# Attention into MoE: the sums of squares move from VectorE and GpSimd to ScalarE and GpSimd

## The chip, the cores and the metric

The kernel runs on one core of a Trainium2 chip. The metric is device time in microseconds (us), lower is better. A core has five engines that run their own instruction queues in order: TensorE (PE, with its weight loads shown as PEld), VectorE (DVE), ScalarE (ACT), GpSimd (POOL) and SyncE (SP), which here issues every DMA.

## The reference

Random-feature attention feeds a mixture of experts. What matters here is the feature map `phi`, made for every row of q and k.

```python
def phi(x):                                   # x: batch 4, heads 8, rows 576, head_dim 64
    proj = np.einsum('bhsd,md->bhsm', x, omega)          # m = 128 features
    sq = np.sum(x * x, axis=-1, keepdims=True) / 2.0
    h = proj - sq
    h = h - np.max(h, axis=-1, keepdims=True)
    return np.exp(h) / np.sqrt(m)
q_p, k_p = (phi(q_s), phi(k_s))               # q_s, k_s = q * scale, k * scale, scale = 64 ** -0.25
kv = np.einsum('bhsm,bhsd->bhmd', k_p, v)
z = np.sum(k_p, axis=2)
num = np.einsum('bhsm,bhmd->bhsd', q_p, kv)
den = np.einsum('bhsm,bhm->bhs', q_p, z)[..., None] + 1e-06
x = num / den                                 # 2304 tokens of 512
# MoE: 8 experts of 512 -> 1024 -> 512, gates normalised by 8 Sinkhorn rounds
for e in range(8):
    out += P[:, e:e + 1] * (np.maximum(x @ w1[e], 0.0) @ w2[e])
```

## The kernel before

**Two parts.** The attention part makes the 2304 tokens and ends at about 175 us. The MoE part, from about 192 us to the end, is a long stream of matmuls of split-precision operands, on 16 units (expert, half of its hidden width).

**Jobs.** Attention is cut into 36 jobs, 0 to 35, written out in `jobs`: 18 k jobs and 18 q jobs. A job takes one half of the heads of one loaded tile (`k`, `q`, or the remainders `kr`, `qr`); a tile of 128x1024 serves two jobs. Jobs 0 to 4 are k jobs, 5 to 30 alternate k and q, 31 to 35 are q jobs. Each runs as a generator whose stages are advanced by `tick`, so several jobs overlap.

**A job on the engines.** PE transposes the tile (`tp`, L327); ACT or DVE copies the result to SBUF (`th`, L330 or L332); PE multiplies by omega (`pp`, L339, 16 matmuls, one such group in each job); DVE takes the negated maxima into one column of `sqs` (L342) and adds the three columns of `sqs` to the shift `cn` (L344); half of the exponentials are made by ACT with that shift as bias (L352), the other half by DVE's addition (L354) and ACT's exponential (L355). A k job then multiplies with v (`kv`, L364); a q job transposes, multiplies with `kvs` and divides.

**The sums of squares.** `squares` writes, for one tile, two columns of `sqs`: the sum of squares times c and times -c (they cancel in the sum of three columns when the maximum, which stands between them, is taken over the projection alone). Tile 0 is squared by ACT (L300). All others are squared by GpSimd (L302) and folded in halves by GpSimd down to 8 columns (L305); DVE ends the sum (L306) and makes the two scaled columns (L307, L308). `ensure_loads` calls `load` and `squares` ahead of the job that needs them.

**What sets the order.** A scheduler that simulates a timeline sets each engine's order from the order of the code and the dependencies; work with no dependency that holds it can be drawn forward. `last_cn` is used for ties: a GpSimd copy of 8 columns of the newest `cn` into a tile makes what fills that tile wait for that job.

**Weights.** `stage` loads weights of a unit, `split` makes their high and low parts (ACT copies `wh`, GpSimd or DVE subtracts to `wl`, L223); unit 0's first weights are handled inside the attention part. The tokens of a chunk (three chunks of 6 tiles) are split by ACT (L125), DVE (L126) and GpSimd (L110) and stored to DRAM as `xd`.

Of the kernel before, what the change touches and what calls it, by code (L numbers as in the profile page):

```python
# [9 lines left out]
F32 = mybir.dt.float32  # L10
F32R = mybir.dt.float32r
AF = mybir.ActivationFunctionType
ALU = mybir.AluOpType
AX = mybir.AxisListType
# [8 lines left out]
def moe_attention_kernel(  # L23
# [23 lines left out]
    nc = tc.nc  # L47
    B, H, S, D = q.shape
    M = omega.shape[0]
    N, DM = out.shape  # L50
    E = w_gate.shape[1]
    FF = w1.shape[2]
    P = 128
    KD = DM // P
# [25 lines left out]
    def bank(name):  # L80
        return ps[0].tile([P, 512], F32, tag="b", name=name)
# [9 lines left out]
    ORDER = [1, 5, 6, 3, 7, 2, 4]  # L91
# [77 lines left out]
    last_cn = []  # L169
# [58 lines left out]
    sc = sc_cm.__enter__()  # L228
    rw_cm = tc.tile_pool(name="rw", bufs=1, side="right", reuse_waits="tile")
    rw = rw_cm.__enter__()  # L230
# [12 lines left out]
    wgs = sc.tile([P, KD, GC], F32, name="wgs")  # L243

    def prepare_gate():

        nc.gpsimd.memset(wgs, 0.0)
        wg = sc.tile([P, KD, E], F32, name="wg")
        nc.sync.dma_start(out=wg, in_=w_gate.rearrange("(k p) e -> p k e", p=P))
        nc.vector.tensor_copy(wgs[:, :, :E], wg)  # L250

    rawt = {}
    vts = [rw.tile([P, H, 2 * D + 2], F32, name=f"v{i}") for i in range(4)]
    for t in vts:
        nc.gpsimd.memset(t[:, :, 0 :: 2 * D + 1], 1.0)
    nv = [0]

    def load(which, key):

        src = {"q": q, "k": k, "v": v}[which]  # L260
        is_v = which == "v"
        if key[0] == "r":
            pr = key[1]
            rows = [(slice(i * SR, (i + 1) * SR), 2 * pr + i) for i in range(2)]
            if is_v:
                t = rw.tile([P, H, D + 1], F32, tag="vr", bufs=1, name="vr")
                nc.gpsimd.memset(t[:, :, :1], 1.0)
                o = t[:, :, 1:]
            else:
                t = rw.tile([P, H, 1, D], F32, tag=f"{which}r", bufs=1, name=f"{which}r")  # L270
                o = t[:, :, 0, :]
            for r, b in rows:
                nc.sync.dma_start(out=o[r], in_=src[b, :, SM:S, :].rearrange("h p d -> p h d"))
            rawt[which, key] = t
            return
        b, half = key
        view = src[b, :, :SM, :].rearrange("h (p j) d -> p h j d", j=JM)[:, :, 2 * half : 2 * half + 2, :]
        if is_v:
            t = vts[nv[0] % 4]
            nv[0] += 1  # L280
            nc.sync.dma_start(out=t[:, :, 1 : 2 * D + 1].rearrange("p h (j d) -> p h j d", j=2), in_=view)
        else:
            t = rw.tile([P, H, 2, D], F32, tag=which, bufs=4, name=which)
            nc.sync.dma_start(out=t, in_=view)
        rawt[which, key] = t

    sqt = {}
# [3 lines left out]
    def squares(which, key):  # L291

        t = rawt[which, key]
        n = 1 if key[0] == "r" else 2
        s = sc.tile([P, H, n, D], F32, tag="sq", bufs=2, name="sq")
        o = sc.tile([P, H, n, 3], F32, tag="sqs", bufs=8, name="sqs")
        c = 1.0 / (2.0 * math.sqrt(D))
        w = D
        if not sqt:
            nc.scalar.activation(s, t[:, :H], AF.Square)  # L300
        else:
            nc.gpsimd.tensor_tensor(s, t[:, :H], t[:, :H], op=ALU.mult)  # L302
            while w > 8:
                w //= 2
                nc.gpsimd.tensor_tensor(s[..., :w], s[..., :w], s[..., w : 2 * w], op=ALU.add)  # L305
        nc.vector.tensor_reduce(o[..., 1], s[..., :w], axis=AX.X, op=ALU.add)  # L306
        nc.vector.tensor_scalar_mul(o[..., 0], o[..., 1], c)  # L307
        nc.vector.tensor_scalar_mul(o[..., 2], o[..., 1], -c)  # L308
        sqt[which, key] = o

    kvs = {}
# [8 lines left out]
    def feature_stages(which, key, hh, on_act):  # L320


        tin = rawt[which, key].rearrange("p h j d -> p (h j d)")
        tp = bank("tp")
        for i in range(4):
            o = (4 * hh + i) * P
            nc.tensor.transpose(tp[:, i * P : (i + 1) * P], tin[:, o : o + P], ident)  # L327
        th = sc.tile([P, 4, P], F32, tag="th", bufs=2, name="th")
        if which == "k" and len(sqt) > 4:
            nc.scalar.copy(th.rearrange("p a s -> p (a s)"), tp)  # L330
        else:
            nc.vector.tensor_copy(th.rearrange("p a s -> p (a s)"), tp)  # L332
        yield
        hs = sqt[which, key].rearrange("p h j t -> p (h j) t")[:, 8 * hh : 8 * hh + 8]
        pp = [bank("pp") for _ in range(2)]
        for i in range(4):
            for g in range(2):
                r = slice(g * D, (g + 1) * D)
                nc.tensor.matmul(pp[g][:, i * M : (i + 1) * M], lhsT=th[r, i], rhs=omt[r], start=True, stop=True)  # L339
        p3 = [p.rearrange("p (h m) -> p h m", h=4) for p in pp]  # L340
        for g in range(2):
            nc.vector.tensor_reduce(hs[:, g::2, 1], p3[g], axis=AX.X, op=ALU.max, negate=True)  # L342
        cn = sc.tile([P, 8], F32, tag="cn", bufs=4, name="cn")
        nc.vector.tensor_reduce(cn, hs, axis=AX.X, op=ALU.add)  # L344
        last_cn.append(cn)
        res = []
        for g in range(2):
            ex = sc.tile([P, 4, M], F32, tag="ex", bufs=8, name="ex")
            c4 = cn[:, g::2]
            if on_act and g == 1:  # L350
                for i in range(4):
                    nc.scalar.activation(ex[:, i, :], p3[g][:, i, :], AF.Exp, bias=c4[:, i : i + 1])  # L352
            else:
                nc.vector.tensor_tensor(ex, p3[g], c4.unsqueeze(2).to_broadcast([P, 4, M]), op=ALU.add)  # L354
                nc.scalar.activation(ex, ex, AF.Exp)  # L355
            res.append(ex)
        yield
        yield
        return res
# [370 lines left out]

    def ensure_loads(i):
        for it in list(need):
            if it[0] <= (i + 1 if it[1] == "v" else i + 3):
                need.remove(it)
                load(it[1], it[2])
                if it[1] != "v":
                    sq_todo.append(it)
        while sq_todo and sq_todo[0][0] <= i + 2:
            _, w, key = sq_todo.pop(0)
            squares(w, key)  # L740

    sq_todo = []
# [9 lines left out]

    ensure_loads(0)
    for i, jb in enumerate(jobs):
        if i == 4:
            prepare_gate()
        if i == 8:
            stage(0, 1)
        if i >= 14 and i % 2 == 0 and (i - 14) // 2 < 7:
            split(0, 1, ORDER[(i - 14) // 2])  # L760
        if i == 24:
            stage(0, 2)
        gen = k_job(jb[1], jb[2]) if jb[0] == "k" else q_job(*jb[1:])
        active.append((jb, gen))
        tick()
        ensure_loads(i + 1)
# [25 lines left out]
    for s, (u, n) in enumerate(steps):  # L792
        c = n // (CT // 2)
# [11 lines left out]
        for k, i in enumerate(ORDER):  # L805
# [3 lines left out]
            if k < ((5, 5, 4) if s > 2 else (3, 4, 3))[n % 3] and todo:  # L809
                pc = todo.pop(0)  # L810
                first(*pc)
                j = ORDER.index(pc[2])
# [44 lines left out]
```

## Time and profile before

| what | value |
| --- | --- |
| time, three runs | 1652.38, 1653.94, 1654.0 us; median 1653.94 us |
| the profiled execution | 1653.92 us, with a span of 1652.1 us from its first to its last instruction |
| PE busy | 96% of the span |
| DVE busy | 85% |
| ACT busy | 46% |
| POOL busy | 19% |

The shares are means over both parts. The MoE part is nearly all of the span, so they say little of the attention part, in which each engine's share is a different one.

### The profile page before, as it was taken

How to read it: one execution, taken by the hardware profiler on the slowest of the kernel's cores; microseconds unless marked ns; L12 is line 12 of the kernel's file. 1: busy time of each engine (PE TensorE's matmuls, PEld its weight loads, DVE VectorE, ACT ScalarE, POOL GpSimd, SP SyncE). 2: the span in 40 equal slices, each digit the busy share in tenths (PEclk: the TensorE clock that was granted, in tenths of full speed). 3: DMA queues.
4: the chain of work that ended last, by engine and by line, in shares of the span. 5: the costliest groups of instructions: out<-in, count | busy, mean ns of one | idle time of the engine just before them, and what ended most of it. 6: DMA issues, size and time to landing. Idle time of an engine off the chain costs nothing.

```text
span 1652.1 us, 31432 instructions
## 1 busy us (share of the span) xinstructions
PE 1591.1 (96%) x12318; PEld 1556.0 (94%) x12318; DVE 1412.3 (85%) x2779; ACT 759.9 (46%) x1373; POOL 316.9 (19%) x259
## 2 busy tenths in 40 slices
PE   5799889999999999999999999999999999999998
PEld 4678679999999999999999999999999999999997
DVE  6988779898979898889888888989898888889877
ACT  2577655444434344443544443444444444444333
POOL 7871141111102011111111120102111111101003
PEclk8899999999999999999999999999999999999999
DMA  9423576665665655566657565665665565655562
GB/s 231 110 83 137 207 282 238 201 221 172 239 208 198 210 204 206 209 217 215 218 175 256 169 219 200 218 210 206 209 218 206 203 229 184 214 189 192 176 226 77
DMA packets 105314, 329.79 MB, mean 200 GB/s; under 512 B 14800, under 2 KB 43984, under 8 KB 105168
## 3 DMA queue, kind: packets, MB, share of 16 engines
q1 hardware_dynamic: 105168, 327.79, 58.5%
q8 instruction: 98, 1.61, 0.4%
q14 instruction: 48, 0.39, 0.1%
HBM read 306.53 MB, written 21.23 MB: 198 GB/s over the span
## 4 chain that ended last, share of the span: by engine, by line
PE 82%; DVE 12%; POOL 2%; DMA 1%; issue 1%; ACT 1%; SPq 0%; DVEq 0%; ACTq 0%; POOLq 0%
PE hx L553 23%; PE x L654 22%; PE hz L553 17%; PE z L654 11%; PE w L654 5%; PE pp L339 2%; DVE out L680 2%; DVE sm L590 2%; DVE sqs L342 1%; DVE bl L590 1%; DVE wl L223 1%; POOL sq L305 1%; DVE sl L629 1%; POOL sq L302 1%; PE np L439 1%
## 5 line engine op out<-in xcount | busy, mean ns | idle before, releaser
L553 PE MATMUL hx<-xs,wh 128*128 128x384 f32 x1536 | 373.2, 337 | 2.0 <-ACT xs L125 1.4
L680 DVE SCALAR_TENSOR_TENSOR out<-x,prob,out 128x256 f32<-128x256 f32 x497 | 233.3, 476 | 66.2 <-PE x L654 64.7
L553 PE MATMUL hz<-xs,wh 128*128 128x384 f32 x1152 | 281.0, 336 | 3.5 <-ACT hr L572 1.4
L553 PEld LDWEIGHTS hx<-xs,wh 128*128 128x128 f32 x1536 | 270.1, 189 | 4.3 <-issue 3.7
L190 POOL TENSOR_TENSOR st<-st 128x512 f32<-128x512 f32 x80 | 131.9, 1649 | 702.3 <-DVE wl L223 699.7
L553 PEld LDWEIGHTS hz<-xs,wh 128*128 128x128 f32 x1152 | 202.2, 188 | 4.9 <-ACT hr L572 1.6
L553 PE MATMUL hx<-xs,wl 128*128 128x384 f32 x768 | 199.7, 336 | 0.0
L632 ACT ACTIVATE bh<-hr 128x512 fp32r<-128x512 f32 x144 | 91.2, 634 | 223.2 <-PE x L654 218.2
L680 DVE SCALAR_TENSOR_TENSOR out<-z,prob,out 128x256 f32<-128x256 f32 x252 | 120.0, 476 | 58.0 <-PE z L654 57.2
L222 ACT CAST wh<-st 128x512 fp32r<-128x512 f32 x176 | 105.0, 621 | 112.7 <-PE hx L553 45.0
L628 ACT CAST sh<-sm 128x512 fp32r<-128x512 f32 x144 | 89.6, 622 | 139.0 <-PE z L654 99.3
L553 PE MATMUL hz<-xs,wl 128*128 128x384 f32 x576 | 150.4, 335 | 0.0
L553 PEld LDWEIGHTS hx<-xs,wl 128*128 128x128 f32 x768 | 139.0, 189 | 0.0
L590 DVE SCALAR_TENSOR_TENSOR sm<-hr,sm 128x256 f32<-128x256 f32 x288 | 135.0, 469 | 2.7
L223 DVE TENSOR_TENSOR wl<-st,wh 128x512 fp32r<-128x512 f32 x169 | 120.6, 724 | 15.1 <-ACT wh L222 14.7
L590 DVE SCALAR_TENSOR_TENSOR bl<-hr,bh 128x512 fp32r<-128x512 f32 x144 | 119.1, 827 | 3.5 <-ACT bh L632 3.3
L654 PE MATMUL z<-wh,sh 128*128 128x256 f32 x576 | 117.7, 281 | 2.8 <-ACT sh L611 2.7
L654 PE MATMUL x<-wl,sh 128*128 128x256 f32 x576 | 118.3, 281 | 0.0
L654 PE MATMUL x<-wh,sh 128*128 128x256 f32 x576 | 117.5, 285 | 0.7 <-DVE out L680 0.6
L654 PE MATMUL z<-wh,sl 128*128 128x256 f32 x576 | 115.5, 282 | 1.6 <-DVE sl L612 1.6
L602 ACT ACTIVATE ah<-hr 128x256 fp32r<-128x256 f32 x144 | 60.3, 419 | 123.3 <-PE x L654 98.0
L654 PE MATMUL z<-wl,sh 128*128 128x256 f32 x576 | 117.0, 281 | 0.0
(155 smaller groups left out, 3507.8 us busy)
## 6 DMA issues: line engine op xcount, KB each, us to landing
xs<-xd SPq DMA_DIRECT2D x329, 768.0 KB, 4.4
st<-in_moe_w_dram SPq DMA_DIRECT2D x64, 512.0 KB, 4.8
xd<-xs SPq DMA_DIRECT2D x21, 768.0 KB, 4.3
k<-in_k_dram SPq DMA_DIRECT2D x8, 512.0 KB, 6.3
v<-in_v_dram SPq DMA_DIRECT2D x8, 512.0 KB, 6.2
q<-in_q_dram SPq DMA_DIRECT2D x8, 512.0 KB, 6.3
out_dram<-out SPq DMA_DIRECT2D x32, 128.0 KB, 1.9
kr<-in_k_dram SPq DMA_DIRECT2D x4, 128.0 KB, 5.8
```

What stands on the lines that cost most here:

```text
L190: nc.gpsimd.tensor_tensor(o, a, b, op=op)
L222: nc.scalar.copy(hi, o)
L223: (nc.vector if u > 0 or (w == 2 and i in (1, 6, 7, 4)) else nc.gpsimd).tensor_tensor(lo, o, raw(hi), op=ALU.subtract)
L302: nc.gpsimd.tensor_tensor(s, t[:, :H], t[:, :H], op=ALU.mult)
L339: nc.tensor.matmul(pp[g][:, i * M : (i + 1) * M], lhsT=th[r, i], rhs=omt[r], start=True, stop=True)
L553: nc.tensor.matmul(pb, lhsT=a[:, k, g * P : (g + 1) * P], rhs=x[:, b, k, :], start=i in (1, 5, 2) and j == 0, stop=j == len(prods) - 1, sk ...
L590: nc.vector.scalar_tensor_tensor(o, in0=a, scalar=0.0, in1=b, op0=ALU.max, op1=op)
L602: nc.scalar.activation(ah, a11, AF.Relu)
L628: nc.scalar.copy(sh, sm)
L632: nc.scalar.activation(bh, a[:, 1:], AF.Relu)
L654: nc.tensor.matmul(pb, lhsT=ops[s][i][a][:, f], rhs=wt[u, 2, i][b][:, f], start=bool(start) and j == 0, stop=j == len(prods) - 1, skip_gro ...
L680: nc.vector.scalar_tensor_tensor(o, in0=pb, scalar=p, in1=o, op0=ALU.mult, op1=ALU.add)
```

## The change

- `squares`: every tile is squared by ACT (L298 in the new file), with a scale that puts the factor c into the square. GpSimd folds from 64 columns down to 2 (L302), adds the last two straight into `sqs` (L303) and writes the negated column (L304). DVE has no part in it. From the first `cn` on, a GpSimd copy (L297) from the newest `cn` into the tile `sq` stands ahead of ACT's square: the tie.
- `feature_stages`: all copies `th` of k jobs are ACT's; the first four were DVE's.
- `ensure_loads`: loads are called for 2 jobs ahead (v) and 5 (q, k) in place of 1 and 3; squares 2 ahead up to job 7, then 4.
- The weights of unit 0: `stage(0, 1)` moves from job 8 to 16, the seven `split` calls from jobs 14 to 26 to jobs 22 to 34, `stage(0, 2)` from job 24 to 30.
- The gate weights are loaded straight into `wgs`, at job 12; the tile `vr` is made and its ones set once.

```diff
@@ def prepare_gate
-        wg = sc.tile([P, KD, E], F32, name="wg")
-        nc.sync.dma_start(out=wg, in_=w_gate.rearrange("(k p) e -> p k e", p=P))
-        nc.vector.tensor_copy(wgs[:, :, :E], wg)
+        nc.sync.dma_start(out=wgs[:, :, :E], in_=w_gate.rearrange("(k p) e -> p k e", p=P))
@@ def squares
-        o = sc.tile([P, H, n, 3], F32, tag="sqs", bufs=8, name="sqs")
-        c = 1.0 / (2.0 * math.sqrt(D))
+        o = sc.tile([P, H, n, 3], F32, tag="sqs", bufs=10, name="sqs")
+        if last_cn:
+            nc.gpsimd.tensor_copy(s.rearrange("p h j d -> p (h j d)")[:, :8], last_cn[-1])
+        nc.scalar.activation(s, t[:, :H], AF.Square, scale=1.0 / math.sqrt(2.0 * math.sqrt(D)))
         w = D
-        if not sqt:
-            nc.scalar.activation(s, t[:, :H], AF.Square)
-        else:
-            nc.gpsimd.tensor_tensor(s, t[:, :H], t[:, :H], op=ALU.mult)
-            while w > 8:
-                w //= 2
-                nc.gpsimd.tensor_tensor(s[..., :w], s[..., :w], s[..., w : 2 * w], op=ALU.add)
-        nc.vector.tensor_reduce(o[..., 1], s[..., :w], axis=AX.X, op=ALU.add)
-        nc.vector.tensor_scalar_mul(o[..., 0], o[..., 1], c)
-        nc.vector.tensor_scalar_mul(o[..., 2], o[..., 1], -c)
+        while w > 2:
+            w //= 2
+            nc.gpsimd.tensor_tensor(s[..., :w], s[..., :w], s[..., w : 2 * w], op=ALU.add)
+        nc.gpsimd.tensor_tensor(o[..., :1], s[..., :1], s[..., 1:2], op=ALU.add)
+        nc.gpsimd.tensor_scalar_mul(o[..., 2], o[..., 0], -1.0)
@@ def feature_stages
-        if which == "k" and len(sqt) > 4:
+        if which == "k":
@@ def ensure_loads
-            if it[0] <= (i + 1 if it[1] == "v" else i + 3):
+            if it[0] <= (i + 2 if it[1] == "v" else i + 5):
...
-        while sq_todo and sq_todo[0][0] <= i + 2:
+        while sq_todo and sq_todo[0][0] <= i + (2 if i < 8 else 4):
@@ the loop over jobs
-        if i == 4:
+        if i == 12:
             prepare_gate()
-        if i == 8:
+        if i == 16:
             stage(0, 1)
-        if i >= 14 and i % 2 == 0 and (i - 14) // 2 < 7:
-            split(0, 1, ORDER[(i - 14) // 2])
-        if i == 24:
+        if i >= 22 and i % 2 == 0 and (i - 22) // 2 < 7:
+            split(0, 1, ORDER[(i - 22) // 2])
+        if i == 30:
             stage(0, 2)
```

**GpSimd, the first squares.** Before, from its 16th row on: `sq<-k`, `sq<-kr` and `sq<-q` are the products, `sq<-sq` the folds.

```order
L302 TENSOR_TENSOR sq<-k 128x1024
L305 TENSOR_TENSOR sq<-sq 128x16x32
L302 TENSOR_TENSOR sq<-kr 128x512
L305 TENSOR_TENSOR sq<-sq 128x16x16
L305 TENSOR_TENSOR sq<-sq 128x8x32
L305 TENSOR_TENSOR sq<-sq 128x16x8
L305 TENSOR_TENSOR sq<-sq 128x8x16
L302 TENSOR_TENSOR sq<-k 128x1024
```

The same place on GpSimd now, where `sqs<-sq` is the last sum, `sqs<-sqs` the negation and `sq<-cn` a tie.

```order
L302 TENSOR_TENSOR sq<-sq 128x16x8
L304 TENSOR_SCALAR sqs<-sqs 128x16
L302 TENSOR_TENSOR sq<-sq 128x16x4
L297 COPY sq<-cn 128x8
L302 TENSOR_TENSOR sq<-sq 128x16x2
L303 TENSOR_TENSOR sqs<-sq 128x16
L304 TENSOR_SCALAR sqs<-sqs 128x16
L302 TENSOR_TENSOR sq<-sq 128x8x32
```

The products have left this engine, short operations have come, and each later chain stands behind a tie. Up to the exponentials of job 8 twelve tiles are squared in the order of before, and eight now.

**ScalarE, jobs 0 to 2.** Before, from the first square on:

```order
L300 ACTIVATE sq<-k 128x1024
L352 ACTIVATE ex<-pp,cn 128x128 x4
L355 ACTIVATE ex<-ex 128x512
L352 ACTIVATE ex<-pp,cn 128x128 x4
L355 ACTIVATE ex<-ex 128x512
L352 ACTIVATE ex<-pp,cn 128x128 x4
L355 ACTIVATE ex<-ex 128x512
L330 COPY th<-tp 128x512
```

ScalarE now, from the same row on:

```order
L298 ACTIVATE sq<-k 128x1024
L326 COPY th<-tp 128x512
L298 ACTIVATE sq<-k 128x1024
L326 COPY th<-tp 128x512
L348 ACTIVATE ex<-pp,cn 128x128 x4
L298 ACTIVATE sq<-kr 128x512
L351 ACTIVATE ex<-ex 128x512
L326 COPY th<-tp 128x512
L348 ACTIVATE ex<-pp,cn 128x128 x4
L298 ACTIVATE sq<-k 128x1024
L351 ACTIVATE ex<-ex 128x512
```

A square stands between the two kinds of exponential of a job, or ahead of the copy `th` of the next.

**SyncE, the stores of the first two chunks.** Before, `xd` are the stores of tokens and `st` the loads of weights:

```order
L128 DMA xd_7_1866<-xs 128x1536
L128 DMA xd_2_1923<-xs 128x1536
L128 DMA xd_4_2008<-xs 128x1536
L182 DMA st<-in_moe_w_dram 128x2x512
L128 DMA xd_1_2550<-xs 128x1536
L128 DMA xd_5_2611<-xs 128x1536
```

SyncE now, at the same place:

```order
L128 DMA xd_7_1882<-xs 128x1536
L128 DMA xd_2_1945<-xs 128x1536
L128 DMA xd_4_2032<-xs 128x1536
L182 DMA st<-in_moe_w_dram 128x2x512 x4
L128 DMA xd_1_2587<-xs 128x1536
L128 DMA xd_5_2648<-xs 128x1536
```

Four weight loads now stand between the stores of the first chunk and those of the second; before it was one, and three stood further ahead.

## Rows read from the trace of the kernel before

**Rows 1.** The page: the span.

```profile
span 1652.1 us, 31432 instructions
```

**Rows 2.** Stretches: length, engines' busy us (instructions), granted clock, DMA share, GB/s.

```profile
8.92:59.41 50.49, 31.82 (x393) 26.78 (x393) 40.75 (x70) 14.57 (x41) 44.97 (x50) 0.80 0.80 178
59.41:108.31 48.90, 44.91 (x781) 39.80 (x781) 44.58 (x117) 38.46 (x102) 33.85 (x34) 1.00 0.34 91
108.31:152.62 44.31, 40.99 (x551) 34.97 (x547) 35.82 (x80) 30.92 (x74) 20.68 (x22) 0.88 0.52 179
152.62:173.51 20.89, 20.15 (x305) 17.79 (x305) 17.97 (x47) 15.11 (x42) 0.00 (x0) 1.00 0.01 3
173.51:245.00 71.49, 57.95 (x438) 50.66 (x438) 54.17 (x86) 40.76 (x78) 24.75 (x15) 0.95 0.69 270
...
108.31:129.89 21.58, 18.94 (x202) 15.26 (x199) 15.76 (x32) 14.04 (x29) 16.01 (x18) 0.76 0.60 196
```

The engines in these rows are PE, PEld, DVE, ACT, POOL, in this order.

**Rows 3.** Timeline of PE: the groups `pp` of jobs 0, 8, 21, 30, 35.

```profile
8.92 2.08 PE L339 MATMUL pp<-omt,th 64*128 64x128 f32 x16 [1.92 <-DVE th L332]
...
59.41 1.16 PE L339 MATMUL pp<-omt,th 64*128 64x128 f32 x16 [1.08 <-DVE th L332]
...
108.31 1.16 PE L339 MATMUL pp<-omt,th 64*128 64x128 f32 x16
...
152.62 1.16 PE L339 MATMUL pp<-omt,th 64*128 64x128 f32 x16 [0.17 <-DVE cn L344]
...
173.51 1.71 PE L339 MATMUL pp<-omt,th 64*128 64x128 f32 x16
```

**Rows 4.** Waits of PE and ACT in 0 to 60: total us, times, longest.

```profile
PE pp L339 <- DVE th L332: 12.7, 6, 4.4
...
ACT ex L352 <- DVE cn L344: 34.3, 8, 7.4
```

**Rows 5.** Timeline of GpSimd and VectorE near 16 us: start, length.

```profile
16.30 1.89 POOL L302 TENSOR_TENSOR sq<-k 128x1024 f32<-128x1024 f32 x1
16.35 1.89 DVE L308 TENSOR_SCALAR sqs<-sqs 128x16 f32<-128x16 f32 x1
```

**Rows 6.** Groups by line and form, VectorE, 0 to 175 us.

```profile
L308 DVE TENSOR_SCALAR sqs<-sqs 128x16 f32<-128x16 f32 x16 | 14.9, 933 | 0.0
L332 DVE COPY th<-tp 128x512 f32<-128x512 f32 x22 | 14.9, 679 | 0.0
...
L307 DVE TENSOR_SCALAR sqs<-sqs 128x16 f32<-128x16 f32 x16 | 10.4, 650 | 0.3
...
L306 DVE TENSOR_REDUCE sqs<-sq 128x16 f32<-128x128 f32 x15 | 4.2, 282 | 6.5 <-POOL sq L305 6.5
...
L308 DVE TENSOR_SCALAR sqs<-sqs 128x8 f32<-128x8 f32 x4 | 0.6, 160 | 0.0
```

**Rows 7.** Groups by line and form, GpSimd, 0 to 135 us.

```profile
L305 POOL TENSOR_TENSOR sq<-sq 128x512 f32<-128x512 f32 x15 | 19.0, 1267 | 0.2
L302 POOL TENSOR_TENSOR sq<-q 128x1024 f32<-128x1024 f32 x8 | 15.2, 1900 | 9.1 <-DMA q<-in_q_dram 3.8 <-DVE sqs L306 2.8 <-DVE cn L344 2.5
L305 POOL TENSOR_TENSOR sq<-sq 128x256 f32<-128x256 f32 x19 | 14.6, 768 | 0.3
L302 POOL TENSOR_TENSOR sq<-k 128x1024 f32<-128x1024 f32 x7 | 13.3, 1897 | 9.8 <-DMA k<-in_k_dram 7.8 <-DVE sqs L306 2.0
L305 POOL TENSOR_TENSOR sq<-sq 128x128 f32<-128x128 f32 x19 | 8.7, 462 | 0.2
...
L305 POOL TENSOR_TENSOR sq<-sq 128x64 f32<-128x64 f32 x4 | 1.3, 317 | 0.2
```

**Rows 8.** Groups by line and form, ScalarE, 0 to 245 us.

```profile
L222 ACT CAST wh<-st 128x512 fp32r<-128x512 f32 x18 | 10.6, 623 | 10.8 <-POOL st L190 7.0 <-DMA st<-in_moe_w_dram 3.8
...
L330 ACT COPY th<-tp 128x512 f32<-128x512 f32 x14 | 8.4, 603 | 2.3 <-PE tp L327 2.1
...
L300 ACT ACTIVATE sq<-k 128x1024 f32<-128x1024 f32 x1 | 1.1, 1057 | 0.1
```

More of the change, by code (lines that the diff above doesn't have):

```diff
@@ L256, in moe_attention_kernel @@
     nv = [0]
+    vrt = rw.tile([P, H, D + 1], F32, name="vr")
+    nc.gpsimd.memset(vrt[:, :, :1], 1.0)
     def load(which, key):
@@ L265, in load @@
             if is_v:
-                t = rw.tile([P, H, D + 1], F32, tag="vr", bufs=1, name="vr")
-                nc.gpsimd.memset(t[:, :, :1], 1.0)
+                t = vrt
                 o = t[:, :, 1:]
```

## The prediction

> **What bounds the kernel now.** I read the page first: the profiled execution took 1653.92 us, with a span of 1652.1 us [rows 1], so 1.8 us lie around it, and the median of the runs (1653.94 us) is the same time. All sums below are made against 1653.9 us. About 0.2% of it, 3.3 us, is what a measurement can tell from no change.
>
> Then I cut the attention part at the matmul groups `pp`, of which each job has one: they start at 8.92 us (job 0), 59.41 (job 8), 108.31 (job 21), 152.62 (job 30) and 173.51 (job 35) [rows 3]. This gives a pace. Jobs 8 to 21 take 48.9/13 = 3.76 us each, jobs 21 to 30 take 4.9, jobs 30 to 35, all q jobs with more matmuls, 4.2. Jobs 0 to 8, mostly k jobs with fewer matmuls, take 50.5/8 = 6.3. The first jobs should be the quickest and are the slowest. That is stage A; B is jobs 8 to 21, C is 21 to 30, D is 30 to 35, E is what follows to 245 us.
>
> The stretches say who is full in each stage [rows 2]. In A GpSimd is busy 45.0 of 50.5 us and VectorE 40.8, while PE has 31.8 and ScalarE only 14.6. In B PE and VectorE are equally full (44.9 and 44.6 of 48.9). In C PE is first (41.0 of 44.3). From 175 us on nothing of the change runs. So what can be won lies in A, and A's waits point back to VectorE: ScalarE waits 34.3 us in 60 for `cn`, PE 12.7 us for the copy `th` that stands in VectorE's queue [rows 4].
>
> Why VectorE is full there can be seen in two neighbouring rows [rows 5]. A scaling of 16 columns (L308) starts at 16.35 us, 0.05 us after a GpSimd product of 1.89 us, and ends with it: it also takes 1.89. Where nothing runs beside it this form takes 0.16 us [rows 6]. Over 16 tiles L307 and L308 take 10.4 + 14.9 = 25.3 us, against 32 x 0.16 = 5.1 undisturbed: 20 us in which VectorE stands still beside GpSimd. The Trainium skill ("SBUF — State Buffer", Who interferes with whom) calls this an exclusive lock on a shared port pair, held for a whole instruction; the rows above agree.
>
> **The change, part by part.**
>
> *VectorE* loses L306 (4.2 us), L307 and L308 (25.3 us) on the 16 large tiles, 29.5/16 = 1.84 us a tile [rows 6], and four of the 22 copies `th` at 0.68. In A that is eleven tiles by the order (20 us) and two copies there (1.4): 40.8 - 21.6 = about 19 us of work are left.
>
> *GpSimd.* A large tile cost 1.90 + 1.27 + 0.77 + 0.46 = 4.40 us [rows 7]. Now the product is gone, the three folds stay (2.50), and five short operations come: a fold to 4 columns (64 elements, a form that takes 0.317), one to 2, the last sum, the negation and the tie. From 128 to 64 elements the price falls from 0.462 to 0.317, so by the same line 32, 16 and 8 elements take some 0.25, 0.21 and 0.19; an upper bound is 0.317 for each. A tile then takes 2.50 + 0.32 + 0.25 + 0.21 + 0.21 + 0.19 = 3.68 us, at most 4.09. What decides more is how many tiles stand in A: the order shows twelve squared before job 8's exponentials, and only eight now, since the tie holds each one back. Seven large ones and one small (about 2.4) make 28 us in place of 45.
>
> *ScalarE* gets squares of 1.06 us [rows 8]: six in A after job 0's exponentials (one is small), so 5.9 us, and two copies `th` at 0.60: 14.6 + 7.1 = 21.7 us. In B about six squares (6.4) come and four weight copies at 0.62 go: 38.5 + 3.9 = 42.4 of 48.9. In C four to five squares and two weight copies: 30.9 + 6 = 37 of 44.3. In D two weight copies, 15.1 + 1.2. It fits, but ScalarE goes from under 80% to near 87% in B.
>
> *The end of A.* No engine keeps more than PE's 31.8 us, and those contain groups at the half clock (the group `pp` takes 2.08 us at 8.92 and 1.16 at 59.41 [rows 3]; the granted clock in A is 0.80 [rows 2], a mean of the levels 1.2 and 2.4 GHz). So A cannot get below GpSimd's 28 us, a gain of 22 us; nor, if GpSimd still has twelve tiles in A, gain more than 12 x (4.40 - 3.68) = 9, or 12 x 0.31 = 4 with the upper price. I take 32.5 us, about 4.1 a job: near PE's work, because eight jobs of chained steps (transpose, copy, matmul, maximum, shift, exponential) rarely go faster than their fullest engine, and well over ScalarE's and VectorE's. That is 18 us won. What is late next is PE.
>
> *B and C.* B is paced by PE (44.9); VectorE's relief can give at most 4 us; I take 1, as ScalarE's new work sits between the two exponentials of a job. C holds three slow jobs at its head: 108.31 to 129.89, 21.6 us at a granted clock of 0.76 [rows 2], where B's pace would need 11.3. Less of VectorE's standing still, and the first splits now spread over jobs 22 to 34, could remove a part; ScalarE's 37 us leave at most 7. I take 2, between none and that, nearer to none because the token work of the first chunk is in this place before and after.
>
> *At nothing:* the loads called earlier stand behind the same buffers in SyncE's queue, and nothing in A is held by them once the first tiles are in (DMA share 0.80 over A, 0.34 in B [rows 2]); if that cover went, one tile's load would show, a few us. The gate weights and `vr` save one short operation each. Of the moved weights, the last copy stands in the order near job 32, some 10 us ahead of the second chunk's tokens; behind it on SyncE's queue are four weight loads and then those tokens' stores, so if the split came late the stores would too. Cover: jobs 32 to 35, about 13 us at 4.2 each. D and E stay, give or take 3.
>
> Sum: 1653.9 - 18 - 1 - 2 = 1632.9, so 1633 us.
>
> **The rivals.**
>
> *GpSimd stays the bound in A.* For it: 45 of 50.5 us busy, more instructions a tile than before, and now a column that VectorE's sum needs comes out of its queue, behind other tiles' folds. Against it: eight tiles, not twelve. Gain 4 to 9 us, about 1647 us. The Trainium skill ("Perfetto Trace Analysis", Optimizing Scalar/DVE Operations) warns that offloading between these two engines may not help, since they share a port. By that rule the moved sums would win nothing; the time would be this rival's, as the product leaves GpSimd in any case.
>
> *ScalarE becomes the bound: slower than before.* ScalarE runs in order. Each of the 18 tied squares waits for GpSimd's copy, which itself waits for a `cn` and behind the folds ahead of it; behind the square wait the exponentials of the same job, and PE's `kv` matmuls for them. If GpSimd is one tile behind each time, that is up to 3.7 us of standing still a square. Room on ScalarE in B, C and D is 6.5 + 7 + 4.6 = 18 us, and A's gain is 18. So from 36/18 = 2 us a square on the kernel gets slower; at 3 us, 54 - 36 gives 1672 us. Against it: the tie's `cn` is one that ScalarE's exponentials just ahead of the square need as well, and they take longer than the copy; GpSimd is busy only 33.9 of 48.9 us in B.
>
> *The late split delays the second chunk.* If the last weight loads reach the queue more than 13 us after job 32, its stores wait for a load and the MoE part starts later, by up to some 8 us: 1641 us. The order speaks against it.
>
> **How the numbers follow.** Forecast (12 to 32 us less, most of it in A) 0.73, with a range of its own of 1622 to 1642; GpSimd still the bound 0.14; late split 0.05; ScalarE the bound 0.06; no change at all (the maxima, not the squares, pace stage A) 0.02. The range is 1622 to 1649: the lower end adds A's bound of 22 us and most of what B and C allow, the upper end takes in GpSimd's case at the upper price; outside are the slow case, no change and a few in a hundred below. Faster by over 0.2%: the forecast, the late split and nearly all of GpSimd's case, less a little for work that I have not seen, 0.87; within 0.2%: 0.06; slower: 0.07.
>
> **What would show it.** Job 8's group `pp` starts near 41 us, not 59; L304 on GpSimd is short and VectorE has no operation of 16 columns stretched to 1.9 us; ScalarE's wait for `cn` in the first 60 us falls by more than half; squares on ScalarE take 1.06 us and wait little for GpSimd; jobs 8 to 21 keep a pace of 3.7; everything from 245 us on is the same, shifted. The prediction is wrong if ScalarE's squares wait long for GpSimd, if job 8 starts after 50 us, or if what is won by job 8 is lost again by job 35.

## The result and the profile after

The changed kernel takes 1634.23 us (median of four runs, 1633.24 to 1634.54), before 1653.97 on the same chip: a ratio of 0.9882, 95% interval 0.9865 to 0.9899. The forecast was 1633. All attributions below go by one profiled execution of each kernel, spans 1652.1 and 1632.6 us. Twenty executions of the kernel before on one chip lie between 1650.4 and 1658.8 us, so a difference of 1 or 2 us between two single traces, with no cause to be seen in them, may be chance.

The stretches of the changed kernel, cut as in [rows 2] at the groups `pp` of jobs 0, 8, 21, 30 and 35; the last one runs from the first expert matmul to the end. Columns: length, then PE, PEld, DVE, ACT, POOL busy, granted clock, DMA share, GB/s.

```profile
7.57:43.02 35.45, 28.22 (x393) 24.00 (x393) 18.27 (x36) 21.10 (x50) 21.12 (x49) 0.95 1.17 246
43.02:93.99 50.97, 46.09 (x782) 40.46 (x781) 38.65 (x95) 42.69 (x107) 31.53 (x75) 1.00 0.38 100
93.99:136.19 42.20, 38.23 (x551) 32.65 (x547) 36.06 (x74) 35.52 (x80) 34.37 (x47) 0.92 0.42 156
136.19:157.08 20.89, 20.15 (x305) 17.79 (x305) 17.99 (x47) 16.47 (x45) 8.40 (x16) 1.00 0.20 69
175.73:1632.60 1456.87, 1436.43 (x10105) 1426.02 (x10105) 1255.98 (x2438) 645.02 (x1089) 207.81 (x137) 1.00 0.60 208
```

With [rows 2, 3] this gives where the 19.5 us of span went: start -1.35, A -15.0 (50.49 to 35.45), B **+2.1** (48.90 to 50.97), C -2.1, D 0, from job 35 to the first expert matmul -0.5 (19.13 to 18.65), the MoE part -2.6 (1459.46 to 1456.87). In A VectorE fell from 40.8 to 18.3 us of work, GpSimd from 45.0 to 21.1, and ScalarE rose from 14.6 to 21.1: the fullest engine is now PE, with 28.2 of 35.5 us. The earlier start is tile 0's sum: before, it stood in VectorE's queue for 1.22 us (L306 at 6.95 us) ahead of job 0's `th`.

Waits of the changed kernel in 0 to 43 us, first ScalarE's, then PE's, then VectorE's (total us, times, longest):

```profile
ACT ex L348 <- DVE cn L340: 4.7, 4, 2.4
ACT sq L298 <- POOL sq L297: 4.2, 3, 1.6
```

```profile
PE kv L360 <- ACT ex L351: 3.9, 2, 2.4
PE pp L335 <- ACT th L326: 1.4, 2, 0.7
```

```profile
DVE sqs L338 <- PE pp L335: 21.4, 7, 9.7
```

ScalarE waited 34.3 us for `cn` in [rows 4], now 4.7; PE's 12.7 us for VectorE's `th` are gone; VectorE itself now waits for PE. New is ScalarE's wait for GpSimd's tie. GpSimd's short operations cost this, by line and form in 0 to 135 us (busy, mean ns, idle before):

```profile
L302 POOL TENSOR_TENSOR sq<-sq 128x64 f32<-128x64 f32 x18 | 6.4, 355 | 1.2
L302 POOL TENSOR_TENSOR sq<-sq 128x32 f32<-128x32 f32 x18 | 4.4, 243 | 1.2
L303 POOL TENSOR_TENSOR sqs<-sq 128x16 f32<-128x16 f32 x15 | 4.1, 271 | 1.0
L304 POOL TENSOR_SCALAR sqs<-sqs 128x16 f32<-128x16 f32 x15 | 4.1, 271 | 1.1
L297 POOL COPY sq<-cn 128x8 f32<-128x8 f32 x17 | 3.3, 191 | 9.6 <-DVE cn L340 9.6
```

And the place where B loses time, the timeline just after job 8's `pp` at 43.02 (start, length, engine, and in brackets the idle time before and who ended it):

```profile
44.92 0.22 POOL L303 TENSOR_TENSOR sqs<-sq 128x16 f32<-128x16 f32 x1
45.23 0.27 POOL L304 TENSOR_SCALAR sqs<-sqs 128x16 f32<-128x16 f32 x1
...
45.43 0.19 POOL L297 COPY sq<-cn 128x8 f32<-128x8 f32 x1
...
45.65 1.06 ACT L298 ACTIVATE sq<-k 128x1024 f32<-128x1024 f32 x1 [1.33 <-POOL sq L297]
...
46.62 0.61 ACT L351 ACTIVATE ex<-ex 128x512 f32<-128x512 f32 x1
...
47.28 0.85 PE L360 MATMUL kv<-v,ex 128*64 128x65 f32 x21 [1.90 <-ACT ex L351]
```

The tie copy takes 0.19 us, but it stands behind the last sum and the negation of the tile before. Behind the tie waits a square for a later job, behind that the exponential of a job in work, and behind that PE. The next `pp` comes at 48.88, 5.9 us after job 8's.

### The profile page after: what moved, and what is told of

It reads as the page before. It is cut to its first block, busy times and chain, and to the rows that moved or that the text cites. A ratio compares the mean times of both kernels' runs of the same rounds, so it can differ in the third digit from the quotient of the medians.

```text
span 1632.6 us, 31484 instructions
## 1 busy us (share of the span) xinstructions
PE 1584.5 (97%) x12318; PEld 1551.6 (95%) x12318; DVE 1379.9 (85%) x2714; ACT 777.3 (48%) x1396; POOL 312.4 (19%) x340
## 4 chain that ended last, share of the span: by engine, by line
PE 86%; DVE 7%; ACT 2%; POOL 2%; DMA 2%; issue 1%; SPq 0%; DVEq 0%; ACTq 0%; POOLq 0%
PE hx L549 24%; PE x L650 23%; PE hz L549 18%; PE z L650 11%; PE w L650 6%; PE pp L335 2%; DVE out L676 1%; DVE sm L586 1%; POOL sq L302 1%; DVE bl L586 1%; DVE sqs L338 1%; PE kv L360 1%; DVE xs L126 1%; ACT ex L348 0%; DMA xs<-xd 0%
```

## The experiments

The theory after the result: the sums of squares paced stage A through VectorE, the tie keeps early squares out of the way, and the rest of the change carries little. Open were why VectorE mattered (it stands still beside GpSimd, as the prediction had it, or it waits in order for GpSimd's sums), where B's 2.1 us came from, and what the moved splits, loads and copies do. In this table, stretches as above, in us:

| kernel | time, ratio [interval] | A | B | C | job 35 to experts | MoE |
| --- | --- | --- | --- | --- | --- | --- |
| before | | 50.5 | 48.9 | 44.3 | 19.1 | 1459.5 |
| changed | 1634.2, 0.9882 [0.9865, 0.9899] | 35.5 | 51.0 | 42.2 | 18.7 | 1456.9 |
| e1 | 1645.9, 0.9951 [0.9935, 0.9967] | 49.7 | 48.8 | 41.3 | 19.3 | 1456.5 |
| e5 | 1651.7, 0.9988 [0.9974, 1.0001] | 43.1 | 54.1 | 46.3 | 19.9 | 1457.9 |
| e6 | 1657.8, 1.0023 [1.0012, 1.0034] | 35.1 | 73.1 | 41.4 | 18.7 | 1457.9 |
| e8 | 1633.9, 0.9876 [0.9860, 0.9893] | 37.6 | 47.8 | 42.2 | 19.3 | 1456.4 |
| e7 | 1638.8, 0.9905 [0.9889, 0.9920] | 32.8 | 47.9 | 45.9 | 18.7 | 1460.0 |
| e10 | 1655.6, 1.0009 [0.9999, 1.0018] | 50.5 | 52.2 | 41.8 | 19.2 | 1459.5 |
| e11 | 1652.6, 0.9992 [0.9980, 1.0003] | 42.8 | 53.7 | 46.9 | 18.7 | 1458.4 |
| e3 | 1643.5, 0.9929 [0.9916, 0.9942] | 33.9 | 61.0 | 42.7 | 18.7 | 1456.8 |
| e4 | 1636.3, 0.9902 [0.9885, 0.9919] | 35.5 | 46.6 | 43.5 | 18.6 | 1462.4 |
| e13 | 1632.4, 0.9877 [0.9857, 0.9898] | 35.2 | 47.5 | 41.8 | 20.2 | 1456.7 |
| e15 | 1632.4, 0.9876 [0.9858, 0.9893] | 36.9 | 46.8 | 43.5 | 18.6 | 1456.0 |
| e16 | 1627.2, 0.9847 [0.9829, 0.9866] | 30.6 | 46.8 | 43.8 | 18.7 | 1455.5 |

D is 20.8 to 21.3 us in all of them. Each ratio is to the kernel before on the same chip.

**e1, the changed kernel without the tie.**

```diff
-        if last_cn:
-            nc.gpsimd.tensor_copy(s.rearrange("p h j d -> p (h j d)")[:, :8], last_cn[-1])
```

> The changed kernel without the ties; 15 tiles are then squared before job 8's exponentials in the order, in place of 8. Theory (stage A is paced by how many tiles GpSimd must fold in it): 15 x 3.7 = 55 us of folding stand in A, job 8's pp starts at 50 us or later, and the time is 1642 to 1655 us. Rival (taking VectorE's operations away is all that counts): job 8 stays near 43 us and the time at 1634 us, give or take 3.

Without the tie A takes 49.7 us, as long as before, and the kernel gains 0.5% in place of 1.2%. Fifteen tiles are squared before job 8's exponentials. The stretch, and ScalarE's two largest waits in 0 to 58 us:

```profile
7.58:57.28 49.70, 35.29 (x393) 29.99 (x393) 17.71 (x35) 26.76 (x57) 38.14 (x92) 0.69 0.82 182
```

```profile
ACT sq L296 <- DMA k<-in_k_dram: 11.6, 3, 7.5
ACT sq L296 <- POOL sqs L301: 8.6, 4, 2.9
```

VectorE is as relieved as in the changed kernel (17.7 us of work), and A is no shorter. A square drawn forward stands in ScalarE's queue until its tile has been loaded, or until GpSimd has folded the tile whose buffer `sq` it needs, with other jobs' copies `th` and exponentials behind it. The theory's time came out, but not its reason: it counted 55 us of folding, and GpSimd is busy for 38.1 of the 49.7. The tie is worth 12 of the 20 us.

**e5, the changed kernel with VectorE ending the sum.**

```diff
-        while w > 2:
+        while w > 8:
...
-        nc.gpsimd.tensor_tensor(o[..., :1], s[..., :1], s[..., 1:2], op=ALU.add)
-        nc.gpsimd.tensor_scalar_mul(o[..., 2], o[..., 0], -1.0)
+        nc.vector.tensor_reduce(o[..., 0], s[..., :w], axis=AX.X, op=ALU.add)
+        nc.vector.tensor_scalar_mul(o[..., 2], o[..., 0], -1.0)
```

> The changed kernel, but GpSimd folds to 8 columns and VectorE ends the sum and negates it (two short operations a tile). Theory (a short VectorE operation that meets a GpSimd fold stands still until it ends): the negation, 0.16 us alone, takes 0.5 us or more on average and up to 1.3; VectorE gets some 15 to 20 us more in 150, job 8 comes 1 to 4 us later, and the time is 1636 to 1642 us. Rival (no standing still, two short operations more are hidden, and GpSimd's shorter chain lets the ties go earlier): 1630 to 1634 us.

Nearly the whole gain is gone, though GpSimd has less to do (16.4 us in A). The stretch, and the timeline near 20 us:

```profile
7.63:50.76 43.13, 28.56 (x393) 23.92 (x393) 19.84 (x49) 21.27 (x50) 16.38 (x26) 0.85 1.03 221
```

```profile
19.62 2.60 POOL L302 TENSOR_TENSOR sq<-sq 128x512 f32<-128x512 f32 x3 [1.95 <-ACT sq L298]
...
22.26 0.29 DVE L303 TENSOR_REDUCE sqs<-sq 128x16 f32<-128x128 f32 x1 [4.10 <-POOL sq L302]
...
22.58 0.18 DVE L304 TENSOR_SCALAR sqs<-sqs 128x16 f32<-128x16 f32 x1
22.66 1.28 DVE L338 TENSOR_REDUCE sqs<-pp 128x4 f32<-128x512 f32 x2
```

Here L304 takes 0.18 us, and in the mean of the 16 large tiles 0.30: it is hardly stretched, as the scalings of [rows 5] were, and the 0.5 us or more of the theory did not come. What costs is the 4.10 us ahead of L303, in which VectorE's queue stands until GpSimd has folded, with the maxima L338 of another job behind. In 0 to 110 us this wait comes to 36.0 us (13 times). With the tie it closes a ring: `cn`, tie, square, folds, VectorE's sum, next `cn`. What the ring adds to the wait was not run by itself (it would need e5 without the tie).

**e11, the changed kernel with the negation alone on VectorE.**

```diff
-        nc.gpsimd.tensor_scalar_mul(o[..., 2], o[..., 0], -1.0)
+        nc.vector.tensor_scalar_mul(o[..., 2], o[..., 0], -1.0)
```

> The changed kernel, with only the negation of the sums given back to VectorE: GpSimd sums down to one column, VectorE multiplies 16 columns by -1. In-order theory: what costs is not the 0.2 us of this operation but its place in VectorE's queue, where it waits until GpSimd has finished the whole chain of a tile (3.3 us of folds and more), with the maxima and shifts of the jobs in work behind it. The time is then 1648 to 1656 us, near the 1651.7 of the kernel in which VectorE did the last sum too, and job 8 starts at 49 to 53 us. Rival (it is the amount of VectorE's and GpSimd's work on the sums that counts, and with it the port): one operation of 0.2 us a tile moves, so 1633 to 1637 us, and job 8 starts before 45 us.

One short operation a tile, handed back, costs 18 us, though the twenty of them are busy for 7.3 us in all (0.38 us in the mean of the large tiles, 0.18 where nothing runs beside it). The time and job 8 (50.21) are those of the in-order theory. Stage A, and VectorE's largest wait in 0 to 50:

```profile
7.46:50.21 42.75, 30.24 (x392) 25.86 (x393) 18.40 (x42) 21.05 (x50) 21.49 (x47) 0.92 0.99 223
```

```profile
DVE sqs L304 <- POOL sqs L303: 19.4, 6, 5.1
```

VectorE and GpSimd have the same work in A as in the changed kernel (18.4 and 21.5 us, against 18.3 and 21.1); only the wait is new.

**e10, the kernel before with the two scalings on GpSimd.**

```diff
-        nc.vector.tensor_scalar_mul(o[..., 0], o[..., 1], c)
-        nc.vector.tensor_scalar_mul(o[..., 2], o[..., 1], -c)
+        nc.gpsimd.tensor_scalar_mul(o[..., 0], o[..., 1], c)
+        nc.gpsimd.tensor_scalar_mul(o[..., 2], o[..., 1], -c)
```

> The kernel before, with only the two scalings of each sum moved from VectorE to GpSimd; GpSimd keeps the product and the three folds, VectorE the sum over 8 columns. This tells how much of stage A was VectorE standing still beside GpSimd's products. Standing-still theory (as the prediction had it): VectorE loses about 21 us of stretched scalings in the first 60 us, GpSimd gains 11 x 0.5 = 5.5 us there; job 8 starts 6 to 12 us earlier, and the time is 1642 to 1648 us. In-order theory (VectorE's sums wait for GpSimd's folds in their queue, and maxima and shifts of other jobs wait behind them; the stretched scalings fill a wait that would be there anyway): VectorE's idle time ahead of its sums grows by what the scalings lose, GpSimd has more to do for each tile, job 8 starts as late as before or later (59 us or more), and the time is 1653 to 1660 us.

This takes away the standing still; the rest of the sums' path stays, with two operations of 0.27 us more on GpSimd for each tile. Stage A, and VectorE's largest wait in 0 to 60:

```profile
8.88:59.41 50.53, 33.05 (x392) 28.55 (x392) 22.75 (x49) 14.40 (x41) 46.67 (x63) 0.76 0.81 186
```

```profile
DVE sqs L306 <- POOL sq L305: 20.3, 5, 6.7
```

VectorE's work in A falls from 40.75 [rows 2] to 22.75 us, and A is as long as before to 0.1 us. Most of the 18 us turned into waiting: VectorE's sums wait 20.3 us for GpSimd's folds, 5.4 before. The stretched scalings filled time in which VectorE would have waited for GpSimd anyway. GpSimd is nearly full here (46.7 of 50.5 us); whether its work or VectorE's waiting for it sets A, the next kernel tells.

**e6, the kernel before with the whole sum on GpSimd**, product, six folds and both scalings; no tie.

```diff
-            while w > 8:
+        while w > 1:
...
-        nc.vector.tensor_reduce(o[..., 1], s[..., :w], axis=AX.X, op=ALU.add)
-        nc.vector.tensor_scalar_mul(o[..., 0], o[..., 1], c)
-        nc.vector.tensor_scalar_mul(o[..., 2], o[..., 1], -c)
+        nc.gpsimd.tensor_scalar_mul(o[..., 0], s[..., 0], c)
+        nc.gpsimd.tensor_scalar_mul(o[..., 2], s[..., 0], -c)
```

> The kernel before, but GpSimd ends and scales the sums itself; products stay on GpSimd, nothing is tied, loads and splits as before. Theory (GpSimd is as much the bound of stage A as VectorE): a tile takes 4.4 + some 1.4 = 5.8 us there, A gets no shorter, the time is 1650 to 1675 us. Rival (VectorE's standing still is the whole of it): A shrinks by 10 us or more, the time is 1636 to 1644 us.

GpSimd has more to do for a tile than before, and is nearly full, yet A takes 35.1 us, as in the changed kernel:

```profile
7.62:42.70 35.08, 28.37 (x393) 24.20 (x393) 20.24 (x39) 14.37 (x41) 33.16 (x57) 1.00 1.15 253
```

VectorE's queue no longer waits for the sums of tiles that no job needs yet, so GpSimd's work on such tiles doesn't set A. A shrinks as the rival said (by e10 not for its reason), but the kernel is 0.2% slower than before: the bill comes in B. The waits in 64 to 87 us:

```profile
ACT wh L222 <- POOL wh L221: 20.5, 1, 20.5
PEld pp L338 <- ACT qt L420: 18.9, 1, 18.9
```

L221 is the tie of a weight copy, which stands behind GpSimd's backlog (it runs at 83.49 us); ScalarE waits for it with `qt` behind, and PE for that. Taking the products off GpSimd shortens this backlog; whether the tie alone would do, with the products left on GpSimd, was not run.

**e8, the kernel before with the new `squares` (tie included) and nothing else of the change.**

```diff
-            nc.gpsimd.tensor_tensor(s, t[:, :H], t[:, :H], op=ALU.mult)
...
+        if last_cn:
+            nc.gpsimd.tensor_copy(s.rearrange("p h j d -> p (h j d)")[:, :8], last_cn[-1])
+        nc.scalar.activation(s, t[:, :H], AF.Square, scale=1.0 / math.sqrt(2.0 * math.sqrt(D)))
...
```

> The kernel before with the new body of squares alone, ties included; copies th, loads, look-ahead and splits as before. Theory (squares and ties carry the gain): job 8's pp starts at 42 to 47 us and the time is 1634 to 1641 us. Rival (earlier loads or later splits carry a large part): 1642 us or more.

1633.9 us: the squares and the tie carry the whole gain. C falls by 2.1 us here too, with the old splits. What the other edits do one by one is hidden in the sum: A is 2.1 us longer than in the changed kernel, B 3.2 us shorter.

**e7, the changed kernel with the tie copied by ScalarE.**

```diff
-            nc.gpsimd.tensor_copy(s.rearrange("p h j d -> p (h j d)")[:, :8], last_cn[-1])
+            nc.scalar.copy(s.rearrange("p h j d -> p (h j d)")[:, :8], last_cn[-1])
```

> The changed kernel, with the eight elements that tie a square to a shift copied by ScalarE itself instead of GpSimd. Theory: in the changed kernel the tied squares wait for GpSimd's copy (4.2 us in the first 43, 2.7 us in jobs 8 to 21) because that copy stands in GpSimd's queue behind the last operations of the tile before, and the exponentials and the `kv` matmuls behind the square wait with it. A copy on ScalarE needs only `cn` and a free `sq` buffer, so these waits go, at a price of some 0.2 us of ScalarE for each of 18 squares; jobs 8 to 21 lose the 2.1 us that they had become longer. The time then is 1630 to 1632 us (2 to 4 less than the changed kernel's 1634.2). Rival: the wait only moves to another place, since a square's buffer comes free when GpSimd has folded the tile two before; the time stays at 1634, within 1 us. Second rival: ScalarE's own copies stand in the way of its exponentials and cost more than the waits; 1636 or more.

```profile
7.96:40.73 32.77, 26.80 (x393) 22.96 (x393) 17.62 (x35) 21.57 (x55) 22.12 (x48) 0.90 1.12 247
40.73:88.58 47.85, 45.49 (x781) 40.21 (x781) 39.22 (x96) 42.83 (x114) 28.45 (x62) 1.00 0.44 118
88.58:134.51 45.93, 38.87 (x551) 32.19 (x547) 35.99 (x74) 35.49 (x84) 33.68 (x43) 0.89 0.38 143
...
174.05:1634.00 1459.95, 1437.08 (x10105) 1426.42 (x10105) 1263.16 (x2438) 643.75 (x1089) 204.68 (x137) 1.00 0.60 207
```

A and B lose 2.7 and 3.1 us against the changed kernel, as the theory said, and the time is still longer: C gives back 3.7, and the MoE part 3.1. Neither was expected. (The trace is of the shortest of four executions, 1635.8 of up to 1640.4 us; 3 us of the distance between the two medians is not in it.) C has the token work of the first chunk and the folds at once, here at a granted clock of 0.89 against 0.92; which of these costs the time is not shown. In the MoE part the written order of TensorE and VectorE is another one to the end, though nothing in its code has changed: the scheduler sets the order of the whole program from its own timeline, and that had moved. VectorE is busy 1263.2 us there for the same 2438 instructions that take 1256.0 in the changed kernel and at most 1258.1 in any kernel but this and e4.

**e3, the changed kernel with the old places of the weights' staging and splits.**

```diff
-        if i == 16:
+        if i == 8:
...
-        if i >= 22 and i % 2 == 0 and (i - 22) // 2 < 7:
-            split(0, 1, ORDER[(i - 22) // 2])
-        if i == 30:
+        if i >= 14 and i % 2 == 0 and (i - 14) // 2 < 7:
+            split(0, 1, ORDER[(i - 14) // 2])
+        if i == 24:
```

> The changed kernel with the weights staged and split as before (stage at jobs 8 and 24, splits from job 14 on, in place of 16, 30 and 22). Theory: the moved splits only carry work from the stretch of jobs 8 to 21 to that of jobs 21 to 35, and what the one gains the other gives: the time stays at 1634 us, within 2 us. Rival: ScalarE is so full with squares in jobs 8 to 21 that four weight copies of 0.62 us more there cost time, some 2 to 5 us: 1636 to 1639 us, with jobs 8 to 21 taking 53 us or more in place of 51.0 and jobs 21 to 35 no less than 62. Second rival: the late split costs time at the start of the second chunk, and the old place is better by 1 to 3 us: 1631 to 1633 us.

None of the three had the 9 us that this costs, nor the cause. All of it is in one gap of 16.2 us, `pp` at 41.49 and 57.70 (5.9 us in the changed kernel):

```profile
49.86 1.26 POOL L190 TENSOR_TENSOR t<-st 128x512 f32<-128x512 f32 x1 [6.87 <-DMA st<-in_moe_w_dram]
...
52.99 0.19 POOL L297 COPY sq<-cn 128x8 f32<-128x8 f32 x1
53.22 1.06 ACT L298 ACTIVATE sq<-k 128x1024 f32<-128x1024 f32 x1 [10.43 <-POOL sq L297]
54.18 0.61 ACT L351 ACTIVATE ex<-ex 128x512 f32<-128x512 f32 x1
...
54.84 1.46 PE L360 MATMUL kv<-v,ex 128*64 128x65 f32 x21 [10.99 <-ACT ex L351]
```

GpSimd's first operation on the weights waits for their load, issued at 39.75, and the tie waits behind it, with ScalarE and PE. In e8, with the same places but the old look-ahead, GpSimd waits only 1.7 us there.

**e4, the changed kernel with the old look-ahead.**

```diff
-            if it[0] <= (i + 2 if it[1] == "v" else i + 5):
+            if it[0] <= (i + 1 if it[1] == "v" else i + 3):
...
-        while sq_todo and sq_todo[0][0] <= i + (2 if i < 8 else 4):
+        while sq_todo and sq_todo[0][0] <= i + 2:
```

> The changed kernel with the look-ahead of before: tiles loaded three jobs ahead and squared two ahead, in place of five and four. Theory: in the changed kernel the first job after job 8 takes 5.9 us (43.02 to 48.88), because a square for a later job, with its tie behind GpSimd's folds, stands in ScalarE's queue ahead of the exponentials that this job needs; with the old look-ahead, as in the kernel before with tied squares, that step takes 3.7 us and jobs 8 to 21 take 48 to 49 us in place of 51.0, so job 35 starts at 154 to 156 us in place of 157.1. The written order of the MoE part on TensorE differs here from that of the changed kernel and is that of the run with ScalarE's tie, where this part took 1460.0 us from the first expert matmul on, against 1456.9. If this order is what costs 3 us there, the time is 1634 to 1637 us; if the 3 us came from elsewhere (the tie, the chip), the MoE part takes 1456 to 1458 us and the time is 1630 to 1633 us. Rival on the look-ahead: it is needed as cover, and without it job 35 starts at 158 us or later.

Job 9 now comes 3.8 us after job 8, B falls from 51.0 to 46.6 us, and job 35 starts at 154.1. The MoE part takes 1462.4 us with the same written order as e7's from early in that part on (VectorE busy 1263.7), and the time is 1636.3. The theory has the cause of B's loss and the time right, the sizes less so: B falls by more than forecast (48 to 49 us), the MoE part is 2.4 us longer than the 1460.0 that it took from e7, and C is 1.3 us longer.

**e13, e15, e16: the tie on ScalarE with the old look-ahead.** e13 is e8 with the tie as in e7; e15 adds the late splits; e16 is the changed kernel with e7's and e4's edits together, so it has e15's and, beside them, the gate weights loaded in place at job 12, `vr` made once, and all `th` of k tiles on ScalarE. Against e8, e13 is:

```diff
-            nc.gpsimd.tensor_copy(s.rearrange("p h j d -> p (h j d)")[:, :8], last_cn[-1])
+            nc.scalar.copy(s.rearrange("p h j d -> p (h j d)")[:, :8], last_cn[-1])
```

> The kernel before with the new squares alone (old look-ahead, loads, copies `th` and splits), and the tie copied by ScalarE instead of GpSimd. The written order of the MoE part is that of the changed kernel. Theory: a square on ScalarE then waits for nothing of GpSimd, jobs 0 to 8 take 33 to 35 us and jobs 8 to 21 at most 47.8; job 35 starts at 152 to 155 us, the MoE part takes 1456.5 us as in the kernels with this order, and the time is 1629 to 1632 us. Rival: what jobs 0 to 21 gain is lost again in jobs 21 to 24, where GpSimd has the token work of the first chunk and the folds at once (as in the changed kernel with ScalarE's tie, 3.7 us): job 35 starts at 156 us or later and the time is 1633 to 1636 us.

> As the run before this one (new squares, tie copied by ScalarE, all else as before), with the weights staged and split late as in the changed kernel. Theory: the late place was worth 9 us in the changed kernel only because GpSimd's first operation on the weights stood there, ahead of a tie, waiting for a load 10 us long; where ties don't stand in GpSimd's queue the place does little: within 1.5 us of the run before this one, 1628 to 1633 us. Rival: the weight copies on ScalarE and VectorE cost time where jobs 8 to 21 are full, and the late place gives 2 to 4 us more, all of it in jobs 8 to 21. Second rival: they come on top of the token work of the first chunk in jobs 21 to 30 and cost 2 to 4 us there.

> The changed kernel with both: the tie copied by ScalarE, and the look-ahead of before. Against the run before this one it adds the gate weights and `vr` without a step between, the gate at job 12 and all copies `th` of k tiles on ScalarE. Theory: these carry nothing: within 1 us of that run, 1628 to 1633 us, with the MoE part at 1456 to 1458 us since its written order is that of the changed kernel. Rival: the copies `th` relieve VectorE in jobs 0 to 8, which then take 1 to 2 us less than in that run.

e13 is between its two cases. Against e8, A is 2.4 us shorter and B and C a little, but the tail (from job 35 to the experts) gives 0.9 back; the ratios to the kernel before, 0.9877 and 0.9876, show no difference. e15 equals e13 in time, as expected: where no tie stands in GpSimd's queue, the late splits do nothing to the total (B 0.7 and the tail 1.5 us shorter, A 1.6 and C 1.7 longer). e16 falls against its theory: it is 5 us faster than e15, all of it in A (30.6 against 36.9, and 35.2 in e13), more than its rival's 1 to 2. The timeline of e13 has a cause for 3 to 4 us, which e8 and e15 have too:

```profile
20.00 0.18 DVE L250 COPY wgs<-wg 128x32 f32<-128x32 f32 x1 [4.32 <-DMA wg<-in_moe_w_gate_dram]
20.09 0.68 DVE L329 COPY th<-tp 128x512 f32<-128x512 f32 x1
...
20.83 1.44 PE L336 MATMUL pp<-omt,th 64*128 64x128 f32 x10 [2.66 <-DVE th L329]
```

The copy of the gate weights waits for its load in VectorE's queue, `th` of job 2 behind it; `pp` starts at 20.83, in e16 at 17.44. The stretches of e16:

```profile
7.80:38.41 30.61, 23.82 (x393) 20.22 (x393) 17.61 (x35) 21.36 (x55) 20.89 (x44) 1.00 1.17 250
38.41:85.23 46.82, 44.85 (x780) 39.86 (x780) 39.29 (x96) 41.00 (x109) 24.20 (x54) 1.00 0.52 131
```

It is the fastest kernel here, below both; its interval just meets that of the changed kernel, and its trace is 8.4 us shorter.

## Why the prediction was right, and where it was not

**Place and size.** The gain was forecast at 21 us, 18 of them in A; the trace has 19.5, 15.0 in A. That the sum came so near is in part luck: A, B and C together give 15.1 of their 21 us, and the other 4.4 come from the start, the MoE part and the stretch before it, which the forecast had at nothing, give or take 3. The busy sums for A came out: 19, 28 and 21.7 us were forecast for VectorE, GpSimd and ScalarE, 18.3, 21.1 and 21.1 measured (GpSimd ended six tiles there; eight were counted). GpSimd's tile costs 3.85 us by the means (1.33 + 0.73 + 0.46 + 0.36 + 0.24 + 0.27 + 0.27 + 0.19) for 3.68. The 0.16 us that the prediction took from [rows 6] for a scaling of 16 columns is that of the form of 8; one of 16 takes 0.17 to 0.18 us where nothing runs beside it (L307 at 8.69 us in the trace of before), which changes its 20 us of standing still by less than one.

**A: 35.5 us, not 32.5.** The squares wait 4.2 us for GpSimd's tie, which the prediction priced only in the slow rival. With the tie on ScalarE (e7) A takes 32.8. Nor was PE's 31.8 us the floor for which it was taken: the same 393 matmuls took 28.2 us at a granted clock of 0.95, against 0.80 before, and 23.8 at 1.00 in e16, where A takes 30.6. The granted clock is not all of it: e13 has 1.00 in A too, and 27.4 us. Nor does it account for the group of 2.08 us at 8.92, which the prediction put down to the half clock: in the trace of before it is 1.00 from 8.92 to 12 us (and 0.50 from 22 to 25 us, where another such group stands).

**B: +2.1, not -1.** The mis-sized term: the pace is 3.92 us a job, where the prediction's sign was 3.7. The mechanism is that of the rival "ScalarE becomes the bound": a tied square behind GpSimd's last operations. It never came near 2 us for each of 18 squares: 6.9 us in five waits over 0 to 94 us, the longest 1.6. But the look-ahead, costed at nothing, put one such square ahead of an exponential that was due. Old look-ahead (e4) or the tie on ScalarE (e7: -1.05, the forecast's own value) each removes it.

**C: -2.1, for -2.** e8 has the same with the old splits, so it does not come from spreading these; e10, which moves only the scalings, has 41.8 us there.

**The reason for A was the wrong one of two.** The prediction took VectorE's 20 us of standing still beside GpSimd for the cause. e10 removes it, and A stays at 50.5 us. What counts is that VectorE's part of a sum waits in its queue for GpSimd's folds, ahead of other jobs' work (e5, e11, and the other way round e6), and that squares run no further ahead than needed (e1). That the place and most of the size came out all the same is luck as far as this reason goes: taking the operations off VectorE took the wait away with them. The Trainium skill ("Perfetto Trace Analysis", Optimizing Scalar/DVE Operations) warns that moving work between VectorE and GpSimd might not help. e10 agrees with it, by another mechanism than the shared port that the page names; e11 shows a move of one short operation a tile that is worth 18 us.

The time of the rival "GpSimd stays the bound in A", 1647 us, came out for the kernel without the tie (e1, 1645.9), where GpSimd has 38.1 us of work in A.

**"At nothing."** The late splits were costed at nothing, with a rival of 8 us lost. They are worth 9 us gained (e3, only beside the new look-ahead), and the gate weights' one short operation stood before a wait of 4.3 us (e13). Both are the same oversight: an operation's price is not its length but what its wait holds up.

**D and E.** D as forecast. The MoE part's -2.6 us lay within the 3 allowed, and its cause is not settled. The written order is not enough: the order of before gave 1459.5 us (before), 1459.5 (e10) and 1457.9 (e5), that of the changed kernel (in some but for a few rows at its start) 1455.5 to 1458.4 in nine kernels. Of before's order e5 lies among the nine and the other two 1 us above them. Only the third order, e7's and e4's (1460.0 and 1462.4), lies above every trace of the other two. Against the spread of executions the -2.6 us is not shown to be an effect of the change.

**Open.** Which step of the MoE part costs the time of e7's order; why C gives back 1.3 to 3.7 us in e7 and e4 (e15 and e16, with late splits as well, have 43.5 and 43.8 there, e13 with the early ones 41.8); what the second half of e16's gain in A is (`th` or the loads; neither was run alone); whether the squares have to move to ScalarE once the tie is there.

## What to carry to other kernels

Before moving an operation, ask what its engine's queue holds behind it while it waits: on an engine that several jobs share, a 0.2 us operation that ends another engine's chain can cost several times its own length (18 us for twenty of them in e11). Let the engine that folds also finish, and hand on only what the next job needs; tie early work to a late event so that it can't be drawn forward. Where the tie stands behind another engine's chain, its wait is passed on (B of the changed kernel, e3); on the engine that does the work the tie shortened A and B, but the total followed only in e16, not in e7 or e13. Where a scheduler writes the order of the whole program, the part that wasn't touched can move by some us too, so compare the parts, not the totals.

## What the runs showed of the hardware that was not expected

GpSimd stands still beside VectorE as well. In e7 the last sum on GpSimd takes 0.97 us while VectorE runs the token split, against 0.22 in the timeline of the changed kernel near 45 us and 0.20 to 0.23 for the other 18 of e7's first 135 us:

```profile
102.04 1.83 DVE L126 TENSOR_TENSOR xs<-xf,xs 128x768 fp32r<-128x768 f32 x2
102.09 0.97 POOL L303 TENSOR_TENSOR sqs<-sq 128x16 f32<-128x16 f32 x1
```

The Trainium skill ("SBUF — State Buffer", Who interferes with whom) says that whichever of the two starts first holds the pair for its whole instruction; both directions now have a row, this one and [rows 5].
